# A spectral filter beside an MLP block on one core: two MLP units queued behind chunk work, norms with a guard column, three warm-up products tied to data

## The chip, the cores and the metric

The kernel runs on one core of one Trainium2 chip. TensorE (PE in the profile; PEld are its weight loads) multiplies, VectorE (DVE), ScalarE (ACT) and GpSimd (POOL) do the elementwise work, and SyncE (SP) issues the DMAs. The metric is device time in microseconds of one execution, the median of three runs.

## What is computed

`x` is 2048 x 448. It is layer-normalised to `xn`, and the output is a sum of three things:

```python
xn = layernorm(x)
y  = irfft2(rfft2(xn) * (w_r + 1j * w_i))          # A: spectral filter
h  = gelu(layernorm(xn) @ w1)                      # B: 448 -> 448
x1 = xn + shift(h) @ w2                            # four column groups, rows shifted by +1 -1 +2 -2
h2 = gelu(layernorm(x1) @ w3) @ w4                 # 448 -> 1792 -> 448
out = x + y + x1 + h2
```

## The kernel before

The 2048 rows are kept as 16 blocks of 128 (row `16 a + b` is partition `a` of block `b`), in four groups of four blocks; group 0 holds blocks 14, 15, 0 and 1. Every large product is made in three passes of f16: high by high, high by low and low by high halves of the two operands. The weights are scaled by powers of two that follow from their sum of squares.

The program runs in stages that overlap.

- **Start** (lines 804 to 867). `warm_up(WARM)` (L806) issues 25 products of a zero tile `wsrc`, 512 columns each, into the bank `wps` (L808), before anything is loaded. `norm1` for group 0 (L328) takes statistics on VectorE (L313, L314), an inverse root by an integer trick (L340, L341) and `nm`, the mean times that root with its sign changed (L343), and applies it to the four blocks: blocks 14 on GpSimd, 15 and 0 on VectorE (L353), block 1 on ScalarE (L350). Meanwhile `squares1` sums the squares of `w1` on ScalarE (L243), one column of `m1` for each of four slices. `powers` (L245) makes the scale of a weight: VectorE sums the columns (`pt`, L248), TensorE sums over partitions with a product by `ones` (`pm`, L254, named p1 for w1), VectorE takes the maximum with 2^-58 (L256) so that a zero matrix gives a usable power, takes the exponent (L258) and builds the scale and its inverse (L260, L261). p1 has the transposes of group 0 behind it (`turn_pe`, L404); `turn_copy` brings them to SBUF as a high half on ScalarE (`xT`, L414) and a low half on VectorE (L415); `split_w` makes the first half of w1 on VectorE (L270); `w1_in` multiplies (L454). `powers` is called four times, for w1, w2, w3 and w4.
- **w1 and w2** for the four groups (L466, L502), the second norm (`ln2`, L508), and the split of w3 and w4.
- **MLP** (`mlp`, L787). The 8 pairs of blocks, G = 0 to 7, are worked in 7 units each, (G, 0) to (G, 6), each over 256 columns of the 1792. `front` (L742) makes the unit's first product (22 products, L425, into a bank `pw`), its gelu in place on ScalarE (L749), the high half `hf` on ScalarE (L752), and the low half on VectorE (L753). `back` (L757) makes the second product from `hf` (12 products, L772, into `acc`). Gs 3 to 5 run beside the chunk stage, with the front of one unit ahead of the back of the unit before; two banks hold `pw` in turn.
- **Chunk stage** (L1011 to L1020): 16 chunks of the spectrum. `chunk_a` transforms along the columns (12 products, `pp`, L648) and halves the result (`pf`, L655 on ScalarE, L656 on VectorE). `chunk_b` makes `px` (6 products, L665), copies it crosswise in two halves on ScalarE (`te`, L670) and multiplies by the filter on VectorE (L671, which reads `px`, then L673); GpSimd adds (`z`, L675). `chunk_z` halves z (`zb`, L682 on ScalarE, L683 on VectorE). `chunk_c` transforms back (`pu`, 12 products, L694) and halves (`y`, L697, L698). `px` and `pu` take turns in two banks, so the px of a chunk needs the bank of the px before it.
- **Inverse transform** beside Gs 6 and 7, and the output.

The order on each engine is set by a planner: it simulates the whole program in time and, on each engine, takes the instruction of the best priority among those that are ready. Inside `with prio(EVAC)` the priority is the best there is, so gelu and halves of a unit run as soon as the simulation has them ready. `with behind(key)` adds an edge of order, with no wait of its own: what is issued inside the block comes after the instruction kept under that key in the queue of the same engine. `behind("te", c)` thus means: on ScalarE after the second copy of te of chunk c, on VectorE after L671 of that chunk. Before the change, there is one such pin in `front`, at L751:

```python
with behind("te", 12) if (G, fp) == (4, 1) else contextlib.nullcontext():
    i = A.activation(out=h[:, 0], in_=pm, func=AF.Copy, scale=h3)
    j = V.scalar_tensor_tensor(out=h[:, 1], ...)
```

Of the kernel before, what the change touches and what calls it, by code (L numbers as in the profile page):

```python
# [12 lines left out]
F32 = mybir.dt.float32  # L13
F16 = mybir.dt.float16
I32 = mybir.dt.int32
AF = mybir.ActivationFunctionType
ALU = mybir.AluOpType
AX = mybir.AxisListType
# [5 lines left out]
CS = {b: 4 * g + i for b, (g, i) in WHERE.items()}  # L24
PASS = ((0, 0), (0, 1), (1, 0))
SHIFT = [1, -1, 2, -2]
WARM = 25
ZPRE = 2.0 ** -7
UPRE = 2.0 ** -3
VPRE = 2.0 ** -3  # L30
# [91 lines left out]
def body(tc, nc, x, wf, w1, w2, w3, w4, c_g, c_n, c_small, out):  # L122
    V, A, P, T, SY = nc.vector, nc.scalar, nc.gpsimd, nc.tensor, nc.sync
# [31 lines left out]
    pc = pool("pc")  # L155
# [8 lines left out]
    def xb(b):  # L164
        g, i = WHERE[b]
        return xt[g][:, i]
# [20 lines left out]
    ones = pc.tile([128, 128], F32, name="ones")  # L187
# [51 lines left out]
    def squares(col, src, junk=None):  # L239

        n = src.shape[-1]
        junk = xr.bitcast(F16) if junk is None else junk
        return A.activation(out=junk[:src.shape[0], :n], in_=src, func=AF.Square, scale=2.0 ** -20, accum_out=col)  # L243

    def powers(m, n, key, tag="acc", mid=None):  # L245

        t = pc.tile([128, 2], F32, name=f"pt{key}")
        i = V.tensor_reduce(out=t[:, 0:1], in_=m[:, :n], axis=AX.X, op=ALU.add)  # L248
        after["t" + key] = (i.ins,)
        if mid:  # L250
            with behind("t" + key):
                mid()
        pm = bank(tag, f"pm{key}") if isinstance(tag, str) else tag
        i = T.matmul(pm[:, 0:1], ones, t[:, 0:1], start=True, stop=True)  # L254
        after["p" + key] = (i.ins,)
        V.tensor_scalar(out=t[:, 1:2], in0=pm[:, 0:1], scalar1=2.0 ** -58, scalar2=None, op0=ALU.max)  # L256
        e = pc.tile([128, 3], I32, name=f"pe{key}")
        V.tensor_scalar(out=e[:, 0:1], in0=t.bitcast(I32)[:, 1:2], scalar1=1, scalar2=0x7F800000,  # L258
                        op0=ALU.logical_shift_right, op1=ALU.bitwise_and)
        V.tensor_scalar(out=e[:, 1:2], in0=e[:, 0:1], scalar1=-1, scalar2=185 << 23, op0=ALU.mult, op1=ALU.add)  # L260
        i = V.tensor_scalar(out=e[:, 2:3], in0=e[:, 0:1], scalar1=1, scalar2=69 << 23, op0=ALU.mult, op1=ALU.add)  # L261
        after["s" + key] = (i.ins,)
        return e.bitcast(F32)[:, 1:2], e.bitcast(F32)[:, 2:3]
# [64 lines left out]
    def norm1(g, apply, seen=0, mid=None):  # L328

        bs = GRP[g]  # L330
        n, b0 = len(bs), bs[0]
        stats1(g, range(seen, n))
        mv = mvs[g]
        a = pc.tile([128, 2 * n], F32, name=f"va{b0}")
        yi = pc.tile([128, 2 * n], I32, name=f"vy{b0}")
        y = yi.bitcast(F32)
        with behind(0, 3) if g == 2 else contextlib.nullcontext():
            V.tensor_scalar(out=a[:, n:], in0=mv[:, :n, 1], scalar1=1.0 + EPS, scalar2=EPS * EPS, op0=ALU.mult, op1=ALU.add)
            V.tensor_scalar(out=a[:, 0:n], in0=mv[:, :n, 1], scalar1=EPS, scalar2=None, op0=ALU.add)
        V.tensor_single_scalar(yi, a.bitcast(I32), 1, op=ALU.logical_shift_right)  # L340
        V.tensor_scalar(out=yi, in0=yi, scalar1=-1, scalar2=0x5F3759DF, op0=ALU.mult, op1=ALU.add)  # L341
        nm = pc.tile([128, n], F32, name=f"nma{b0}")
        i = V.scalar_tensor_tensor(out=nm, in0=mv[:, :n, 0], scalar=-1.0, in1=y[:, n:], op0=ALU.mult, op1=ALU.mult)  # L343
        if mid:
            mid()
        for k, b in enumerate(bs):
            y_, m_ = y[:, n + k:n + k + 1], nm[:, k:k + 1]
            if apply[k] is A:
                with behind("sq", g) if ("sq", g) in after else contextlib.nullcontext():
                    i = A.activation(out=xb(b), in_=xb(b), func=AF.Identity, scale=y_, bias=m_)  # L350
                after["na", g] = (i.ins,)
            else:
                i = apply[k].tensor_scalar(out=xb(b), in0=xb(b), scalar1=y_, scalar2=m_, op0=ALU.mult, op1=ALU.add)  # L353
                after["n" if apply[k] is V else "np", g] = (i.ins,)

        q, z = (pc.tile([128, 2 * n], F32, tag=f"v{t}", bufs=2, name=f"v{t}{b0}") for t in "qz")
        w, r = (pc.tile([128, 2 * n], F32, name=f"v{t}{b0}") for t in "wr")
        nm1 = pc.tile([128, n], F32, name=f"nm{b0}")

        def refine():  # L360
            P.tensor_tensor(out=q, in0=y, in1=y, op=ALU.mult)
            P.tensor_tensor(out=q, in0=q, in1=a, op=ALU.mult)
            P.tensor_scalar(out=w, in0=q, scalar1=-10.0 / 3.0, scalar2=None, op0=ALU.add)
            P.tensor_tensor(out=w, in0=w, in1=q, op=ALU.mult)
            P.tensor_scalar(out=w, in0=w, scalar1=5.0, scalar2=None, op0=ALU.add)
            P.tensor_tensor(out=z, in0=w, in1=w, op=ALU.mult)
            P.tensor_tensor(out=z, in0=z, in1=q, op=ALU.mult)
            P.tensor_scalar(out=z, in0=z, scalar1=-0.5 * 0.375 ** 3, scalar2=1.5 * 0.375, op0=ALU.mult, op1=ALU.add)
            P.tensor_tensor(out=r, in0=z, in1=w, op=ALU.mult)

        def gain():
            i = P.tensor_scalar(out=gsc[:, 4 * g:4 * g + 4], in0=r[:, n:], scalar1=r1, scalar2=None, op0=ALU.mult)
            after["g", g] = (i.ins,)

        def scales():
            c, r1st, u = cs[:, 4 * g:4 * g + 4], w[:, 0:n], w[:, n:]
            P.tensor_tensor(out=r1st, in0=r[:, 0:n], in1=y[:, 0:n], op=ALU.mult)
            P.tensor_tensor(out=u, in0=r[:, n:], in1=r[:, n:], op=ALU.mult)
            P.tensor_tensor(out=c, in0=y[:, n:], in1=a[:, n:], op=ALU.mult)
            P.tensor_tensor(out=c, in0=c, in1=u, op=ALU.mult)  # L380
            P.tensor_tensor(out=c, in0=c, in1=r1st, op=ALU.mult)
            P.tensor_scalar(out=c, in0=c, scalar1=s12[:, 0:1], scalar2=None, op0=ALU.mult)
            P.tensor_tensor(out=nm1, in0=mv[:, :n, 0], in1=r1st, op=ALU.mult)
            P.tensor_scalar(out=nm1, in0=nm1, scalar1=-1.0, scalar2=None, op0=ALU.mult)
            for k, b in enumerate(bs):
                xn_scale[b], xn_bias[b] = r1st[:, k:k + 1], nm1[:, k:k + 1]
        return refine, gain, scales

    after = {}

    @contextlib.contextmanager
    def behind(*key):
        key = key if len(key) > 1 else key[0]
        with contextlib.ExitStack() as st:
            for i in after[key]:
                st.enter_context(tc.issue_after(i))
            yield
# [344 lines left out]
    def front(G, fp, tag):  # L742
        tok = slice(256 * (G % 2), 256 * (G % 2) + 256)
        pm = bank(tag, f"pw3_{G}{fp}")
        for ff in range(2):
            f = 2 * fp + ff
            mlp_in(pm[:, 256 * ff:256 * ff + 256], w3p, slice(128 * f, 128 * f + 128), x2all[:, G // 2], tok)
        with prio(EVAC):
            A.activation(out=pm, in_=pm, func=AF.Gelu_apprx_tanh, scale=r3)  # L749
            h = pw.tile([128, 2, 512], F16, tag="hf", bufs=3, name=f"hf{G}{fp}")  # L750
            with behind("te", 12) if (G, fp) == (4, 1) else contextlib.nullcontext():  # L751
                i = A.activation(out=h[:, 0], in_=pm, func=AF.Copy, scale=h3)  # L752
                j = V.scalar_tensor_tensor(out=h[:, 1], in0=pm, scalar=h3, in1=h[:, 0], op0=ALU.mult, op1=ALU.subtract)  # L753
            after["f", G, fp] = i.ins, j.ins
        hs[G, fp] = h
# [50 lines left out]
    def warm_up(n):  # L806
        for i in range(n):
            T.matmul(wps, wsrc[:, 0:128], wsrc, start=True, stop=True)  # L808

    warm_up(WARM)  # L810
    m1, m2, m3, m4 = (pc.tile([128, n], F32, name=f"m{i}") for i, n in ((1, 4), (2, 1), (3, 4), (4, 7)))
    junk4 = row().bitcast(F16)[:, :2 * D]
    V.memset(m1, 0.0)
    V.memset(m2, 0.0)
    xTs = {}
    flat = lambda t: t.rearrange("p a n -> p (a n)")

# [19 lines left out]
    def squares1():  # L837
# [2 lines left out]
            i = squares(m1[:n, t:t + 1], w1s[:n, t])  # L840
        after["sq", 0] = (i.ins,)

    n1 = [norm1(0, [P, V, V, A], mid=squares1)]
    with behind("n", 0):
        s1, r1 = powers(m1, 4, "1", "mm")
    with behind("p1"):
# [19 lines left out]
    with behind("a0", 1):  # L866
        n1.append(norm1(1, [P, V, A, V]))
    with behind("w1", 3):
        squares(m2[:112], flat(w2s[:112]))
    with behind("n", 1):  # L870
        pts = [turn_pe(1, t) for t in range(2)]
        with behind("T", 1):
# [43 lines left out]
    with behind("w2p"):  # L916
        n1[0][2]()
        n1[1][2]()
        for f in n1[2]:
            f()  # L920
    for b in range(2):
        with behind("T", 2):
# [13 lines left out]
    for b in range(2, 4):  # L936
        w2_tile(b)
    turn(3)
    for f in n1[0]:
        f()  # L940
    ln2([0, 1], [A, P])
    with behind("t", 3), behind("h", 2, 3), behind("b0"):
# [124 lines left out]
```

## Time and profile before

| what | us |
|---|---|
| median of 3 runs | 413.87 (413.73 to 414.08) |
| the profiled execution | 413.43 |
| its span, first to last instruction | 411.7 |
| TensorE busy | 406.6 |
| VectorE busy | 295.9 |
| ScalarE busy | 247.4 |
| GpSimd busy | 115.1 |

A line of the profile's timeline gives the start in us from the span's start, the length in us, the engine, the line of the kernel, the operation, what it writes and reads by the program's names, the shape and, after x, how many instructions are merged in it; the bracket behind it is the idle time of the engine just before and what ended it. Products on TensorE are pipelined: the next starts before the end shown for the last, so the spacing of starts is what a product costs. A line of the waits gives the waiting engine, tile and line, what it waited for, the us in total, the number of waits and the longest.

### The profile page before, as it was taken

How to read it: one execution, taken by the hardware profiler on the slowest of the kernel's cores; microseconds unless marked ns; L12 is line 12 of the kernel's file. 1: busy time of each engine (PE TensorE's matmuls, PEld its weight loads, DVE VectorE, ACT ScalarE, POOL GpSimd, SP SyncE). 2: the span in 40 equal slices, each digit the busy share in tenths (PEclk: the TensorE clock that was granted, in tenths of full speed). 3: DMA queues.
4: the chain of work that ended last, by engine and by line, in shares of the span. 5: the costliest groups of instructions: out<-in, count | busy, mean ns of one | idle time of the engine just before them, and what ended most of it. 6: DMA issues, size and time to landing. Idle time of an engine off the chain costs nothing.

```text
span 411.7 us, 8524 instructions
## 1 busy us (share of the span) xinstructions
PE 406.6 (99%) x3310; PEld 290.2 (70%) x3310; DVE 295.9 (72%) x636; ACT 247.4 (60%) x427; POOL 115.1 (28%) x205
## 2 busy tenths in 40 slices
PE   8999999999999999999999999999999999999996
PEld 3555555765677877776887887777776776677885
DVE  5999999897745658863689889875776787667122
ACT  4697979963738766862678888863343434342321
POOL 2987810112307745400031221111212221221000
PEclk9999999999999999999999999999999999999999
DMA  8979599806911283437066555620000213223001
GB/s 280 363 221 199 99 172 328 188 2 140 175 47 48 88 276 129 131 72 164 13 157 170 146 146 141 158 65 2 2 0 2 68 48 110 91 69 133 24 0 46
DMA packets 53496, 48.53 MB, mean 118 GB/s; under 512 B 37600, under 2 KB 48480, under 8 KB 53456
## 3 DMA queue, kind: packets, MB, share of 16 engines
q1 hardware_dynamic: 53456, 47.99, 43.5%
q8 instruction: 26, 0.43, 0.4%
q14 instruction: 14, 0.11, 0.1%
HBM read 35.52 MB, written 3.67 MB: 95 GB/s over the span
## 4 chain that ended last, share of the span: by engine, by line
PE 91%; ACT 4%; DVE 3%; issue 1%; POOL 0%; DVEq 0%; POOLq 0%
PE pw L425 30%; PE acc L772 29%; PE pw L498 9%; PE pw L454 8%; PE ps L591 3%; PE pe L714 2%; PE py L736 2%; PE wps L808 2%; PE pp L648 2%; ACT te L670 2%; PE pu L694 1%; PE px L665 1%; PE pta L404 1%; DVE te L673 1%; ACT zb L682 1%
## 5 line engine op out<-in xcount | busy, mean ns | idle before, releaser
L425 PE MATMUL pw<-x2mem,w3p 128*128 128x256 f16 x1232 | 149.0, 272 | 0.0
L772 PE MATMUL acc<-w4p,hf 128*128 128x448 f16 (+1 forms) x714 | 138.3, 341 | 0.0
L425 PEld LDWEIGHTS <-w3p 128*128 128x128 f16 x1232 | 118.6, 98 | 18.8
L772 PEld LDWEIGHTS <-hf 128*128 128x128 f16 x714 | 69.4, 98 | 48.2 <-DVE hf L753 0.4
L749 ACT ACTIVATE pw<-pw,pe 128x512 f32<-128x512 f32 x56 | 36.8, 656 | 65.6 <-PE pw L425 65.5
L753 DVE SCALAR_TENSOR_TENSOR hf<-pw,h,hf 128x512 f16<-128x512 f32 x56 | 41.8, 749 | 42.6 <-ACT hf L752 42.2
L498 PE MATMUL pw<-w2p,h 112*128 112x448 f16 x192 | 39.1, 352 | 0.0
L752 ACT ACTIVATE hf<-pw,h 128x512 f16<-128x512 f32 x56 | 38.3, 685 | 1.2
L675 POOL TENSOR_TENSOR z<-te 128x450 f32<-128x450 f32 x16 | 16.0, 1000 | 73.7 <-DVE te L673 73.7
L454 PE MATMUL pw<-w1p,xT 128*128 128x448 f16 x176 | 35.1, 352 | 0.3 <-ACT xT L414 0.3
L721 POOL TENSOR_TENSOR e<-e 128x226 f32<-128x226 f32 x16 | 11.3, 707 | 78.2 <-ACT e L718 75.2
L498 PEld LDWEIGHTS <-h 112*128 112x128 f16 x192 | 18.6, 98 | 16.4 <-DMA h<-x2mem 0.3
L454 PEld LDWEIGHTS <-xT 128*128 128x128 f16 x176 | 17.1, 99 | 16.0 <-ACT xT L414 0.5
L655 ACT ACTIVATE pf<-pp 64x450 f16<-64x450 f32 x32 | 17.3, 541 | 15.8 <-PE pp L648 7.8
L718 ACT ACTIVATE e<-pe 128x452 f32<-128x452 f32 x16 | 8.8, 548 | 26.5 <-PE pe L714 26.5
L656 DVE TENSOR_TENSOR pf<-pp,pf 64x450 f16<-64x450 f32 x32 | 19.9, 622 | 5.3 <-ACT pf L655 5.0
L571 POOL TENSOR_TENSOR xr<-xf 128x452 f32<-128x452 f32 x8 | 9.2, 1153 | 31.1 <-issue 27.7
L670 ACT ACTIVATE te<-px 64x450 f32<-64x450 f32 x32 | 17.2, 539 | 0.5
L729 DVE TENSOR_TENSOR vh<-e,vh 128x448 f16<-128x448 f32 x16 | 10.0, 625 | 9.7 <-ACT vh L728 9.7
L574 POOL TENSOR_TENSOR f<-xr 128x452 f32<-128x452 f32 x16 | 16.1, 1028 | 0.6
L582 DVE TENSOR_TENSOR xh<-f,xh 128x452 f16<-128x452 f32 x16 | 11.8, 782 | 5.0 <-ACT xh L581 5.0
L723 DVE TENSOR_TENSOR e<-e 128x113 f32<-128x113 f32 x16 | 9.5, 594 | 7.8 <-POOL e L721 7.8
(169 smaller groups left out, 603.3 us busy)
## 6 DMA issues: line engine op xcount, KB each, us to landing
wc<-wf SPq DMA_DIRECT2D x32, 225.0 KB, 3.7
wl<-wf SPq DMA_DIRECT2D x8, 450.0 KB, 3.8
xf<-x SPq DMA_DIRECT2D x8, 448.0 KB, 3.6
xt<-x SPq DMA_DIRECT2D x3, 896.0 KB, 11.1
w3raw<-w SPq DMA_DIRECT2D x3, 896.0 KB, 14.1
xr<-x SPq DMA_DIRECT2D x12, 224.0 KB, 2.6
out<-xr SPq DMA_DIRECT2D x12, 224.0 KB, 2.0
gn<-c_g SPq DMA_DIRECT2D x16, 128.0 KB, 3.2
```

The costliest lines, as they stand in the source:

```text
L425: T.matmul(ps_out, wp[:, wi + t, cols], xT[:, xi + t, tok], start=t == 0 and wi + xi == 0, stop=t == 3 and wi == 4)
L454: m = T.matmul(pm[:, :D], xTs[g][:, xi + t, 128 * i:128 * i + 128], w1p[:, wi + t], start=t == 0 and p == 0, stop=t == 3 and p == 2)
L498: m = T.matmul(w2b[b][:, :D], hT[g][:112, 4 * hi + k, o:o + 128], w2p[:, wi, k], start=k == 2 and hi + wi == 0, stop=k == 3 and hi == 1)
L574: P.tensor_tensor(out=f[:, :, k:k + 2].rearrange("p b s d -> p s b d"), in0=u[:, :, 0], in1=u[:, :, 1], op=op)
L655: A.activation(out=hi, in_=src, func=AF.Copy)
L656: V.tensor_tensor(out=lo, in0=src, in1=hi, op=ALU.subtract)
L670: i = A.activation(out=e[64 * h:64 * h + 64], in_=px_[64 - 64 * h:128 - 64 * h, :2 * DF], func=AF.Copy)
L675: P.tensor_tensor(out=z, in0=t[:, 0], in1=t[:, 1], op=ALU.add)
L749: A.activation(out=pm, in_=pm, func=AF.Gelu_apprx_tanh, scale=r3)
L752: i = A.activation(out=h[:, 0], in_=pm, func=AF.Copy, scale=h3)
L753: j = V.scalar_tensor_tensor(out=h[:, 1], in0=pm, scalar=h3, in1=h[:, 0], op0=ALU.mult, op1=ALU.subtract)
L772: m = T.matmul(to, h[:, hi, o:o + 128], w4p[0][:, wi, f, r], start=f == 0 and n == 0, stop=f == 13 and n == 2)
```

## The change

It has four parts.

- In `front`, the gelu of unit (4,1) is put behind te 12, as its halves are already; the halves of unit (4,2) are put behind te 14.
- In `powers`, the tiles `m1` to `m4` get one more column, which holds 2^-65 in all 128 partitions; the sum runs over it, so that the sum over partitions holds 128 x 2^-65 = 2^-58 more. The instruction with the maximum (L256) is gone, and the exponent is taken from the bank itself.
- `WARM` is 22 instead of 25. After the first `norm1` there is `warm_on`: a small f32 product of `ones` with the four columns of `nm` into `wps`, and two warm-up products behind it; then the same with the first four columns of the normalised block 0, and one warm-up product behind it.
- `norm1` hands out `nm` as a fourth result, so its users take the first three.

```diff
-WARM = 25
+WARM = 22
     def powers(m, n, key, tag="acc", mid=None):
-        t = pc.tile([128, 2], F32, name=f"pt{key}")
-        i = V.tensor_reduce(out=t[:, 0:1], in_=m[:, :n], axis=AX.X, op=ALU.add)
+        t = pc.tile([128, 1], F32, name=f"pt{key}")
+        i = V.tensor_reduce(out=t, in_=m[:, :n + 1], axis=AX.X, op=ALU.add)
...
-        i = T.matmul(pm[:, 0:1], ones, t[:, 0:1], start=True, stop=True)
+        i = T.matmul(pm[:, 0:1], ones, t, start=True, stop=True)
         after["p" + key] = (i.ins,)
-        V.tensor_scalar(out=t[:, 1:2], in0=pm[:, 0:1], scalar1=2.0 ** -58, scalar2=None, op0=ALU.max)
         e = pc.tile([128, 3], I32, name=f"pe{key}")
-        V.tensor_scalar(out=e[:, 0:1], in0=t.bitcast(I32)[:, 1:2], scalar1=1, scalar2=0x7F800000,
+        V.tensor_scalar(out=e[:, 0:1], in0=pm.bitcast(I32)[:, 0:1], scalar1=1, scalar2=0x7F800000,
                         op0=ALU.logical_shift_right, op1=ALU.bitwise_and)
...
         with prio(EVAC):
-            A.activation(out=pm, in_=pm, func=AF.Gelu_apprx_tanh, scale=r3)
+            with behind("te", 12) if (G, fp) == (4, 1) else contextlib.nullcontext():
+                A.activation(out=pm, in_=pm, func=AF.Gelu_apprx_tanh, scale=r3)
             h = pw.tile([128, 2, 512], F16, tag="hf", bufs=3, name=f"hf{G}{fp}")
-            with behind("te", 12) if (G, fp) == (4, 1) else contextlib.nullcontext():
+            with behind("te", 10 + 2 * fp) if (G, fp) in ((4, 1), (4, 2)) else contextlib.nullcontext():
                 i = A.activation(out=h[:, 0], in_=pm, func=AF.Copy, scale=h3)
...
-    m1, m2, m3, m4 = (pc.tile([128, n], F32, name=f"m{i}") for i, n in ((1, 4), (2, 1), (3, 4), (4, 7)))
+    m1, m2, m3, m4 = (pc.tile([128, n + 1], F32, name=f"m{i}") for i, n in ((1, 4), (2, 1), (3, 4), (4, 7)))
     junk4 = row().bitcast(F16)[:, :2 * D]
-    V.memset(m1, 0.0)
-    V.memset(m2, 0.0)
+    for m, n in ((m1, 4), (m2, 1), (m3, 4), (m4, 7)):
+        V.memset(m, 0.0)
+        V.memset(m[:, n:], 2.0 ** -65)
...
+    def warm_on(src, n):
+
+        after["on"] = (T.matmul(wps[:, 0:4], ones, src, start=True, stop=True).ins,)
+        with behind("on"):
+            warm_up(n)
+
     n1 = [norm1(0, [P, V, V, A], mid=squares1)]
+    warm_on(n1[0][3], 2)
+    warm_on(xb(0)[:, 0:4], 1)
```

More of the change, by code (lines that the diff above doesn't have):

```diff
@@ L386, in scales @@
                 xn_scale[b], xn_bias[b] = r1st[:, k:k + 1], nm1[:, k:k + 1]
-        return refine, gain, scales
+        return refine, gain, scales, nm
     after = {}
@@ L868, in body @@
     with behind("w1", 3):
-        squares(m2[:112], flat(w2s[:112]))
+        squares(m2[:112, 0:1], flat(w2s[:112]))
     with behind("n", 1):
@@ L918, in body @@
         n1[1][2]()
-        for f in n1[2]:
+        for f in n1[2][:3]:
             f()
@@ L938, in body @@
     turn(3)
-    for f in n1[0]:
+    for f in n1[0][:3]:
         f()
```

## The prediction

> **What bounds the kernel now.** I read the page first: busy times and the chain that ended last.
>
> ```profile
> span 411.7 us, 8524 instructions
> ...
> PE 406.6 (99%) x3310; PEld 290.2 (70%) x3310; DVE 295.9 (72%) x636; ACT 247.4 (60%) x427; POOL 115.1 (28%) x205
> ...
> PE 91%; ACT 4%; DVE 3%; issue 1%; POOL 0%; DVEq 0%; POOLq 0%
> ```
>
> TensorE (PE) is the bound nearly everywhere: 5.1 us of the span are not PE. An edit on another engine is worth only the hole it closes in PE's stream, and a product added to that stream is worth its full length. So I next read PE's own waits.
>
> ```profile
> PE wps L808 <- DVE wsrc L186: 1.2, 1, 1.2
> PE pw L454 <- ACT xT L414: 0.3, 1, 0.3
> PE px L665 <- DVE te L671: 0.2, 1, 0.2
> ```
>
> Three waits: before the first warm-up product, before the first w1 product, and one px product behind te on VectorE (DVE). The second and third lie where the change works: the start, and the chunk stage near 260 us. Ends of products are modelled, so a hole can be longer than the idle that is shown; I measure holes from start to start.
>
> **The start.** PE's timeline, and its weight loads (PEld), one per product:
>
> ```profile
> 6.74 0.15 PEld L808 LDWEIGHTS <-wsrc 128*128 128x128 f16 x1 [0.28 <-issue]
> ...
> 7.17 2.05 PEld L808 LDWEIGHTS <-wsrc 128*128 128x128 f16 x10 [0.28 <-issue]
> ```
> ```profile
> 9.33 0.38 PE L808 MATMUL wps<-wsrc 128*128 128x512 f16 x1
> 9.55 0.28 PE L254 MATMUL pm<-pt,ones 128*128 128x1 f32 x2
> 9.69 1.07 PE L404 MATMUL pta<-ident,xt 128*128 128x128 f32 x8
> 11.03 0.35 PE L454 MATMUL pw<-w1p,xT 128*128 128x448 f16 x1 [0.27 <-ACT xT L414]
> ```
>
> A warm-up product takes 0.43 us (6.74 to 7.17) and from 7.17 on a good half of it, 0.22 us (9.33 to 9.55). The 25 end at 9.55, where the norm's product (p1) starts at once; the transposes of x follow at 9.69. What the data did meanwhile, on DVE and ScalarE (ACT):
>
> ```profile
> 7.63 0.16 DVE L343 SCALAR_TENSOR_TENSOR nma<-mva,vy 128x4 f32<-128x4 f32 x1
> 7.83 1.26 DVE L353 TENSOR_SCALAR xt<-xt,vy,nma 128x448 f32<-128x448 f32 x2
> 9.18 0.16 DVE L248 TENSOR_REDUCE pt<-m 128x1 f32<-128x4 f32 x1
> 9.87 0.16 DVE L256 TENSOR_SCALAR pt<-pm 128x1 f32<-128x1 f32 x1 [0.53 <-PE pm L254]
> 10.06 0.15 DVE L258 TENSOR_SCALAR pe<-pt 128x1 int32<-128x1 int32 x1
> ...
> 10.44 0.45 DVE L270 TENSOR_SCALAR w1p<-w1s,pe 128x448 f16<-128x448 f32 x1
> ```
> ```profile
> 10.36 1.08 ACT L414 ACTIVATE xT<-pta 128x512 f16<-128x512 f32 x2 [0.56 <-PE pta L404]
> ```
>
> p1's operand pt is ready at 9.18 + 0.16 = 9.34, so the queue of warm-up products, not the data, is last by 0.21 us. From there the chain is p1, transposes, ACT's copy xT (L414), first w1 product at 11.03.
>
> *The three products that wait.* The total stays 25, but two small f32 products are new: "on" after the 22nd, reading nm, and "on" two products later, reading the normalised block 0. Their price is that of the norm's own two-pass product, which has one moving column where these have four:
>
> ```profile
> 20.36 0.28 PE L254 MATMUL pm<-pt,ones 128*128 128x1 f32 x2
> 20.50 0.35 PE L454 MATMUL pw<-w1p,xT 128*128 128x448 f16 x1
> ```
>
> 0.14 us of PE's stream here (20.36 to 20.50), and 0.14 at 9.55. I take 0.14 each; as a lower bound 0 if PE would have waited for data anyway, as an upper bound 0.28, the row's whole length. Neither product waits: 22 products end at 9.55 - 3 x 0.22 = 8.90, nm was ready at 7.63 + 0.16 = 7.79; first "on" to 9.04; two products to 9.47; block 0 ready at 7.83 + 1.26 = 9.09; second "on" to 9.61; the last product to 9.83. p1 starts at 9.83 instead of 9.55. Queued behind it are the transposes, then ACT's copy, which already waits 0.56 for them, then everything on PE. **+0.28 us** (bounds 0 to +0.56).
>
> If the 22 products ended early, data would bind instead: the second "on" at 9.09, p1 at 9.09 + 0.14 + 0.22 = 9.45, against pt at 9.34 before; the term would be +0.11. I don't take it, since in these rows the queue is last.
>
> The two speeds bear on a rule of the Trainium skill, "TensorE: Matmul & The Clock Gate", section "What's actually happening": PE starts at half clock and is released by an activity window that runs free of the kernel's start, so the switch comes at another time in another execution. The trace agrees on a switch at about half the time (0.43 to 0.22 us); that it moves, no run here shows. By that rule an execution with an earlier switch would have the term +0.11 in place of +0.28, and the sum would be -0.54.
>
> *The maximum removed.* In the four norms DVE loses one instruction between the norm's product and the exponent, 10.06 - 9.87 = 0.19 us each. At the first norm it cannot be seen: the half of w1 (L270) would end at 10.44 + 0.45 - 0.19 + 0.28 = 10.98, ahead of the copy that now lets the w1 product start at 11.03 + 0.28 = 11.31. It hides behind transposes and copy; without that cover it would be worth at most 0.19. The other three norms have no PE wait behind them in the list above: 0. The sum over one more column, and six more memsets on DVE while it still waits for x: 0.
>
> **The chunk stage.** Sixteen pairs of L670 (the two copies of te on ACT), of which the last belongs to chunk 15; counting back, 258.33 is te 12 and 267.70 is te 14. The halves that the old pin puts behind te 12 are those at 259.45: unit (4,1). The next are (4,2).
>
> ```profile
> 257.04 0.66 ACT L749 ACTIVATE pw<-pw,pe 128x512 f32<-128x512 f32 x1
> 257.73 0.58 ACT L682 ACTIVATE zb<-z 128x450 f16<-128x450 f32 x1
> 258.33 1.09 ACT L670 ACTIVATE te<-px 64x450 f32<-64x450 f32 x2
> 259.45 0.69 ACT L752 ACTIVATE hf<-pw,h 128x512 f16<-128x512 f32 x1
> ```
> ```profile
> 265.30 0.69 ACT L752 ACTIVATE hf<-pw,h 128x512 f16<-128x512 f32 x1
> ...
> 267.70 1.09 ACT L670 ACTIVATE te<-px 64x450 f32<-64x450 f32 x2
> ```
> ```profile
> 259.46 0.69 DVE L671 SCALAR_TENSOR_TENSOR te<-px,sc,wc 128x450 f32<-128x450 f32 x1 [0.49 <-ACT te L670]
> ...
> 268.83 0.69 DVE L671 SCALAR_TENSOR_TENSOR te<-px,sc,wc 128x450 f32<-128x450 f32 x1
> 269.43 0.68 DVE L673 SCALAR_TENSOR_TENSOR te<-te,sc,wc 128x450 f32<-128x450 f32 x1
> ```
>
> Each time L671 follows ACT's second copy at once, and its end frees the bank into which PE writes the next px. PE at these two places, with the pitch of its products from the chain of work:
>
> ```profile
> 259.84 0.27 PE L648 MATMUL pp<-csm,y 113*128 113x113 f16 x2
> 260.20 0.55 PE L665 MATMUL px<-pf,gn 128*128 128x225 f16 x4
> ```
> ```profile
> 268.51 0.83 PE L694 MATMUL pu<-gn,zb 128*128 128x128 f16 x12
> 269.57 0.74 PE L665 MATMUL px<-pf,gn 128*128 128x225 f16 x6 [0.22 <-DVE te L671]
> ...
> 270.47 0.35 PE L772 MATMUL acc<-w4p,hf 128*128 128x448 f16 x1
> ```
> ```profile
> 206.26 0.60 PE pp L648 x12
> ...
> 220.80 0.67 PE pu L694 x12
> ```
>
> Two pp products stream in 2 x 0.05 = 0.10, so the hole before 260.20 is 260.20 - 259.84 - 0.10 = **0.26 us**; L671 of te 12 ended at 260.15. Twelve pu products take 0.67, so the hole before 269.57 is **0.39 us**; L671 of te 14 ended at 269.52.
>
> *gelu (4,1) behind te 12.* The activation of 257.04 leaves its place. The zb then needs its sum z from GpSimd (POOL):
>
> ```profile
> 256.05 0.98 POOL L675 TENSOR_TENSOR z<-te 128x450 f32<-128x450 f32 x1 [4.61 <-DVE te L673]
> ```
>
> ready at 257.03, so zb runs at 257.05 and te 12 at about 257.65, 0.68 earlier; L671 ends at about 259.47, before PE's turn at 259.94. The hole goes whole: **-0.26**. Queued behind te 12 are now gelu and halves: te ends at 258.74, gelu to 259.43, halves from 259.45, as before. No price.
>
> *Halves (4,2) behind te 14.* Another 0.69 leaves the ACT queue before te 14, so te 14 starts at 267.0 or earlier and L671 ends by 268.85, before PE's turn at 268.51 + 0.67 = 269.18 (268.92 with the first hole gone): **-0.39**. Price: the halves move from 265.30 to 268.1, DVE's lower half (0.75 us as in this stage) to some 269.6. Waiting for them are the acc products of (4,2), now at 270.47 and due at 269.82 with both holes gone. It fits by 0.2 us: 0, at most +0.3. After that nothing is late next: no PE wait in the list.
>
> **Sum** against the profiled execution (413.43 us, span 411.7): +0.28 - 0.26 - 0.39 = **-0.37 us**. The profiled execution lies 0.44 below the median of 413.87, so I put the difference on the median: **413.5**. That is 0.09%; a measurement of this kernel can tell about 0.2% (0.83 us) from no change, so the likeliest verdict is "same".
>
> **Rivals.**
> 1. *Data, not the queue, sets p1*: the start costs 0 to +0.11 and the time is 413.2 to 413.35. For it: pt was only 0.21 ahead of the queue. Against: the profiled execution had the queue last. Chance 0.10. (The rule of the Trainium skill's "TensorE: Matmul & The Clock Gate" that is weighed above is one way to it.)
> 2. *The halves of (4,2) take the place of the wait removed.* If te 14 doesn't move and DVE takes L673 first, the lower half runs from 270.11 to 270.86 and acc waits from 270.47 - 0.26 = 270.21 on, 0.65 us, while the second hole stays: +0.28 - 0.26 + 0.65 = +0.67, 414.5; half of it, if DVE takes the half first. It decides when the half ends after 269.8. Against: the 0.69 us freed ahead of te 14. Chance 0.12.
> 3. *Slower: a planner's order.* Order on each engine comes from a simulated timeline of the whole program. DVE's norms get shorter and PE's start longer in it, and gelu and halves of the stage's other units may fall ahead of a te elsewhere. Each such place costs a hole like the two measured, 0.26 to 0.39, at most 0.69, the halves' length. One hole eats the forecast gain; four, 4 x 0.33 = +1.3, make 414.8. For it: two of the last three rounds had one without any pin to avoid it. Against: PE shows no other wait after 11 us. Chance 0.23.
> 4. *The same planner's order closes more than the two holes.* To pass -0.83 another 0.46 would have to go; 412.8 with 0.7. PE's shown idle holds no such wait, only holes under modelled ends. Chance 0.13.
> The forecast has 0.42.
>
> **From these to the numbers.** Faster by over 0.2% (under 413.04): rival 4 and a little of rival 1 and the forecast, 0.16. Slower (over 414.70): most of rival 3 and a little of rival 2, 0.22. Same: 0.62. Range 412.7 to 415.0: it holds all but a third of rival 4 and of rival 3 each, some 0.12, and the bounds of the start (0 to +0.56).
>
> **What would show it.** Start right: p1 at 9.83, first w1 product at 11.31; wrong: p1 at 9.55 or before. Maximum right: DVE's e instruction directly after p1, w1 product still released by ACT's xT. Pins right: te 12 about 0.7 earlier against its px, no PE wait on L671, no start-to-start hole ahead of the px of chunks 13 and 15; wrong: a PE wait on hf L753. The prediction falls if PE's order of stages differs from before, or if PE's total of waits after 12 us is above 0.6 us.

## The result and the profile after

The changed kernel takes 413.27 us in the median (22 runs, 412.89 to 413.85), the kernel before in the same comparison 413.89. The ratio is 0.9981, with a 95% interval of 0.9975 to 0.9987: 0.62 us less by the medians, 0.79 by the ratio. Forecast were 413.5 and -0.37: the sign is right, and the gain is larger than forecast, since the interval of the ratio is -0.54 to -1.03 us (a second comparison, f3_changed_again below, gives -0.32). Two of the 22 runs of the kernel before took 415.42 and 415.57, none of the changed kernel's did; the second group of experiments is about such runs. The profiled execution took 413.19.

The page of the changed kernel: span, busy times, the chain that ended last. Its line numbers are one less than before from `powers` on to `front`.

```profile
span 411.4 us, 8535 instructions
...
PE 406.0 (99%) x3314; PEld 290.1 (71%) x3314; DVE 294.4 (72%) x638; ACT 247.7 (60%) x427; POOL 114.6 (28%) x205
...
PE 93%; DVE 3%; DMA 2%; ACT 1%; POOL 1%; issue 0%
```

In the chunk stage the chain no longer runs through te on ScalarE and VectorE; from 250 to 275 us all of it is on PE. PE's waits say the same:

```profile
PE wps L808 <- DVE wsrc L186: 1.2, 1, 1.2
PE wps L846 <- DVE xt L352: 0.5, 1, 0.5
PE pw L453 <- ACT xT L413: 0.3, 1, 0.3
```

The wait of px for te is gone, and the second tie (L846, reading block 0) has one of its own. PE's timeline at the start:

```profile
1.22 6.60 PE L808 MATMUL wps<-wsrc 128*128 128x512 f16 x22 [1.22 <-DVE wsrc L186]
7.94 0.39 PE L846 MATMUL wps<-nma,ones 128*128 128x4 f32 x2
8.18 0.59 PE L808 MATMUL wps<-wsrc 128*128 128x512 f16 x2
9.24 0.39 PE L846 MATMUL wps<-xt,ones 128*128 128x4 f32 x2 [0.47 <-DVE xt L352]
9.48 0.38 PE L808 MATMUL wps<-wsrc 128*128 128x512 f16 x1
9.70 0.28 PE L254 MATMUL pm<-pt,ones 128*128 128x1 f32 x2
9.84 1.07 PE L403 MATMUL pta<-ident,xt 128*128 128x128 f32 x8
11.16 0.93 PE L453 MATMUL pw<-w1p,xT 128*128 128x448 f16 x4 [0.25 <-ACT xT L413]
```

The 22 products end at about 7.7, not at 8.9 as worked out. With 0.43 us for a cold and 0.22 for a warm product, 6.5 us are some 8 cold ones, where the profile of before had 14: the clock opened after 3.4 us here and after 6.0 us there. So in this execution the data bind: the second tie waits for block 0 until 9.24, p1 starts at 9.70 and the first w1 product at 11.16, 0.13 later than before. The two ties take 0.24 us of the stream each (7.94 to 8.18, 9.24 to 9.48), where the sum had 0.14.

The chunk stage, ScalarE at te 12 and te 14, then PE at the px of chunks 13 and 15:

```profile
257.46 0.58 ACT L681 ACTIVATE zb<-z 128x450 f16<-128x450 f32 x1
257.94 1.08 ACT L669 ACTIVATE te<-px 64x450 f32<-64x450 f32 x2
258.92 0.64 ACT L749 ACTIVATE pw<-pw,pe 128x512 f32<-128x512 f32 x1
```
```profile
265.53 0.55 ACT L654 ACTIVATE pf<-pp 64x450 f16<-64x450 f32 x1 [0.77 <-DVE pf L655]
266.13 0.58 ACT L681 ACTIVATE zb<-z 128x450 f16<-128x450 f32 x1
266.73 0.60 ACT L696 ACTIVATE y<-pu 113x512 f16<-113x512 f32 x1
267.35 1.10 ACT L669 ACTIVATE te<-px 64x450 f32<-64x450 f32 x2
268.48 0.69 ACT L752 ACTIVATE hf<-pw,h 128x512 f16<-128x512 f32 x1
```
```profile
259.55 0.83 PE L693 MATMUL pu<-gn,zb 128*128 128x128 f16 x12
260.22 0.55 PE L664 MATMUL px<-pf,gn 128*128 128x225 f16 x4
```
```profile
268.96 0.83 PE L693 MATMUL pu<-gn,zb 128*128 128x128 f16 x12
269.63 0.74 PE L664 MATMUL px<-pf,gn 128*128 128x225 f16 x6
270.21 0.73 PE L772 MATMUL acc<-w4p,hf 128*128 128x448 f16 x3
```

Twelve pu products last 0.67, and px now follows exactly 0.67 behind them, twice (260.22 - 259.55, 269.63 - 268.96): both holes are closed. Te 12 starts 1.63 us behind its own px (256.31), where it was 2.40 (255.93 to 258.33): 0.77 earlier. The acc products of (4,2) run at 270.21 against 270.47 before. The stage gives 0.64 us: the pu ahead of chunk 13's px, at 259.17 before, comes 0.38 later than there, and acc 0.26 earlier. Of the 0.38, 0.13 is the start; most of the rest is a longer wait of a w2 product near 36 us for a transposing DMA (weight loads: 0.5 us instead of 0.3), which the other profiles below show at all lengths between. The span as a whole is only 0.3 us shorter in this pair of profiles.

The wait "0.77 <-DVE pf" on ScalarE, three instructions ahead of te 14, is one that the prediction did not have, and it matters below. So does a new order on PE between the px of chunk 14 and the pu ahead of chunk 15's px, first before, then after:

```profile
265.29 0.74 PE L665 MATMUL px<-pf,gn 128*128 128x225 f16 x6
265.87 0.73 PE L772 MATMUL acc<-w4p,hf 128*128 128x448 f16 x3
266.44 2.24 PE L425 MATMUL pw<-x2mem,w3p 128*128 128x256 f16 x19
```
```profile
265.23 0.74 PE L664 MATMUL px<-pf,gn 128*128 128x225 f16 x6
265.81 0.92 PE L772 MATMUL acc<-w4p,hf 128*128 128x448 f16 x4
266.56 2.56 PE L424 MATMUL pw<-x2mem,w3p 128*128 128x256 f16 x22
```

One acc and three pw products more stand there, so pu comes 3.73 us behind px instead of 3.22 (268.96 - 265.23, 268.51 - 265.29), and the px of chunk 15 is due 0.51 later.

### The profile page after: what moved, and what is told of

Its sections match the earlier page's. It is cut to its first block, busy times and chain, and to the rows that moved or that the text cites. A ratio compares the mean times of both kernels' runs of the same rounds, so it can differ in the third digit from the quotient of the medians.

```text
span 411.4 us, 8535 instructions
## 1 busy us (share of the span) xinstructions
PE 406.0 (99%) x3314; PEld 290.1 (71%) x3314; DVE 294.4 (72%) x638; ACT 247.7 (60%) x427; POOL 114.6 (28%) x205
## 4 chain that ended last, share of the span: by engine, by line
PE 93%; DVE 3%; DMA 2%; ACT 1%; POOL 1%; issue 0%
PE pw L424 33%; PE acc L772 31%; PE pw L497 8%; PE pw L453 6%; PE pu L693 3%; PE ps L590 3%; PE pp L647 2%; PE pe L713 2%; PE px L664 2%; PE py L735 2%; DMA h<-x2mem 1%; DMA xt<-x 1%; DVE sta L312 1%; PE pta L403 1%; DVE xT L414 0%; DVE xt L352 0%
## 5 line engine op out<-in xcount | busy, mean ns | idle before, releaser
L581 DVE TENSOR_TENSOR xh<-f,xh 128x452 f16<-128x452 f32 x16 | 12.7, 833 | 5.0 <-ACT xh L580 5.0
```

## Experiments

Each kernel ran in five rounds beside the kernel before; the before in the three groups of four had medians of 413.68, 413.65 and 413.68. The theory at the start is the prediction's: the gain is the two holes, the start costs something, the norms nothing.

### The parts alone

**e1_pins**: both pins, nothing else.

```diff
-            A.activation(out=pm, in_=pm, func=AF.Gelu_apprx_tanh, scale=r3)
+            with behind("te", 12) if (G, fp) == (4, 1) else contextlib.nullcontext():
+                A.activation(out=pm, in_=pm, func=AF.Gelu_apprx_tanh, scale=r3)
...
-            with behind("te", 12) if (G, fp) == (4, 1) else contextlib.nullcontext():
+            with behind("te", 10 + 2 * fp) if (G, fp) in ((4, 1), (4, 2)) else contextlib.nullcontext():
```

> The kernel before with the two pins alone (gelu of (4,1) behind te 12, halves of (4,2) behind te 14). Theory A (the two holes before the px of chunks 13 and 15 are the whole gain): both holes gone, no other change of the PE stream, -0.65 us, about 413.2. Rival B (the pins gain nothing that lasts, the gain is made at the start): 413.8 to 413.9. Rival C (the gain comes from the norms with fewer instructions): 413.8 to 413.9 as well.

Measured: 413.08, 0.60 less than before. But 3 of its 12 runs took 414.9 to 415.4, with a granted clock of 0.996 (0.999 or 1.000 in the others), so that the ratio is 0.9992 (0.9976 to 1.0008), which alone doesn't exclude 0. Without the runs at a lower clock on either side the medians are 413.02 and 413.65, and both holes are gone from its profile. So theory A holds for the gain, and B and C fall; "no other change of the PE stream" was a miss, for the order on PE changes here as in the changed kernel (1 acc and 3 pw products more ahead of pu). The profiled execution was one of the three, and shows what they are: first a row of PE's waits, then PE's timeline, then the stretch from 12 to 16 us (PEclk is the third number from the end):

```profile
PE pm L254 <- DVE pt L248: 1.3, 1, 1.3
```
```profile
9.81 0.38 PE L254 MATMUL pm<-pt,ones 128*128 128x1 f32 x2 [1.29 <-DVE pt L248]
10.05 1.07 PE L404 MATMUL pta<-ident,xt 128*128 128x128 f32 x8
11.40 1.51 PE L454 MATMUL pw<-w1p,xT 128*128 128x448 f16 x4 [0.27 <-ACT xT L414]
```
```profile
12.00:16.00 4.00, 4.00 (x18) 2.63 (x17) 4.00 (x8) 2.57 (x6) 3.73 (x7) 0.63 1.00 317
```

Here the clock had opened early, the 25 warm-up products were done by 8.4, and PE sat idle for 1.3 us until pt came. Then, with work at hand again, it ran at half clock: four w1 products take 1.51 us where the changed kernel's take 0.93, and the granted clock is 0.63 of full between 12 and 16. In slices of 0.25 us it is 1.00 until 11.50, 0.67 in the next, about 0.5 up to 15.00 and 1.00 after: half clock for 3.4 us, beginning some 1.8 us after p1 started. A clock of 0.996 over 413.1 us is 1.65 us lost, which agrees. That suggested a purpose of the three tied products that the prediction did not see, and the second group tests it.

**e2_start**: 22 products and the two ties, nothing else (the diff's `WARM`, `warm_on` and its two calls).

> The kernel before with the start alone (22 warm-up products, two small products tied to nm and to block 0, three warm-up products behind them). Theory A: two products more in the PE stream, +0.1 (when the clock opens early and data bind) to +0.28 us (when the queue is last), 414.0 to 414.2. Rival B (tying products to data keeps TensorE from something slower in runs without the profiler): faster by 0.3 or more, 413.6 or less. Rival C: 0.

Measured: 413.81, +0.13 (ratio 1.0005, 0.9995 to 1.0015). Theory A's lower end, but the interval, -0.2 to +0.6 us, tells it neither from +0.28 nor from 0 (rival C); B, as a gain of the median, falls. None of the 11 runs is at 0.996; one, of 414.29, is at 0.998.

**e3_guard**: the column and the removed maximum, nothing else.

> The kernel before with the guard column alone (no maximum on VectorE, one more column in the sum). Theory A: the first norm hides behind transposes and copy (0), but the planner's order between 28 and 95 us changes, and the hole of 0.25 us that the profile after shows ahead of 37.28 (a w2 product waiting for the DMA of h) comes with it: 0 to +0.25, 413.9 to 414.1. Rival C (the shorter norms pay): -0.2 to -0.4, 413.5 to 413.7. Rival B: 0.

Measured: 413.62, -0.06 (ratio 0.9995, 0.9984 to 1.0006). The interval, -0.7 to +0.2 us, excludes neither C's gain nor a small price; the profile is sharper. This part alone makes the planner change the order of PE between 60 and 100 us, and of VectorE and ScalarE from some 30 us on. PE is 0.07 later than before at its w1 products (37.02 against 36.95), and still 0.07 later behind the stretch with the new order (acc at 111.67 against 111.60): the shorter norms and the order are together worth nothing there. The hole ahead of 37.02 is 0.10, so the 0.25 ahead of 37.28 in the changed kernel's profile belongs to that execution.

**e4_no_start**: pins and guard.

> The changed kernel without its start: pins and guard, 25 warm-up products as before. Theory A: faster than the changed kernel by 0.1 to 0.28 us, so -0.7 to -0.9 against before by what was measured for the whole change, 413.0 to 413.2. Rival B: slower than the changed kernel, 413.5 or more. Rival C: as the changed kernel, 413.3.

Measured: 413.04, -0.64 (ratio 0.9981, 0.9972 to 0.9989). Theory A, though the changed kernel (413.27) was measured in another comparison. The parts add up, within their intervals: -0.60 + 0.13 - 0.06 = -0.53, against -0.62 for the whole.

### Does the clock fall back?

**f1_warm18**: e4_no_start with fewer products.

```diff
-WARM = 25
+WARM = 18
```

> Pins and guard, and 18 warm-up products with no tie to data (25 before). The one profile of the pins alone that took 414.93 showed TensorE idle for 1.3 us ahead of the first norm's product and its granted clock at 0.63 from 12 to 16 us. Theory D (the clock falls back when TensorE idles between warm-up and data): the warm-up ends at 6.8 to 8.1, the idle time is 1.3 to 2.6 us in every run, so half of the runs or more show a clock of 0.996 and +1.8 us; the median is about 414.8, or there are two groups at 413.0 and 414.8. Rival E (those runs are a disturbance from elsewhere): about one run in eight as before, median 413.0 to 413.1.

Measured: 7 of 12 runs at 0.996 and 414.59 to 415.33, five at 1.000 and 412.91 to 413.36; median 414.64. Theory D. Its profile, one of the seven, PE's waits and the same stretch:

```profile
PE pm L254 <- DVE pt L248: 2.8, 1, 2.8
```
```profile
12.00:16.00 4.00, 4.00 (x19) 2.60 (x18) 3.97 (x9) 2.44 (x6) 3.42 (x7) 0.67 0.99 321
```

**f2_warm15_tied**: the changed kernel with `WARM = 15`, so 18 products in all.

> The changed kernel with 15 products ahead of the first tie in place of 22, so 18 in all: as many as in the run beside it, but three of them wait for data, with two small products. Theory D: the ties cut the idle time into two pieces of about 1 us and the clock is kept in most runs: median 413.2 to 413.4, at most a quarter of the runs at 0.996. Rival E: as the run beside it, 413.1 with one run in eight above.

Measured: 413.42, 2 of 12 runs at 0.996. The two have clocks of 0.995. As many warm-up products as in f1_warm18, but with ties a sixth of the runs instead of seven in twelve: the way that theory D says, though 7 against 2 of 12 could still be chance. Its profile, at a full clock, has pieces of 1.8 and 0.5 us of idle time, not two of about 1:

```profile
8.19 0.39 PE L846 MATMUL wps<-nma,ones 128*128 128x4 f32 x2 [1.76 <-DVE nma L342]
9.49 0.39 PE L846 MATMUL wps<-xt,ones 128*128 128x4 f32 x2 [0.47 <-DVE pt L248]
```

**f3_changed_again** and **f4_pins_start**: the changed kernel once more, and the same without the guard.

> The changed kernel itself, for comparison on the same chip with its variants. Both theories: 413.2 to 413.3; theory D: no run with a clock of 0.996; rival E: one run in eight.

> The changed kernel without the guard: pins and start. If the hole of 0.2 us ahead of 37.3 (the planner's other order between 28 and 95 us) is the guard's price: 413.0 to 413.1, 0.2 less than the changed kernel. If the guard is worth nothing either way: as the changed kernel, 413.2. Theory D: no run at 0.996.

Measured: 413.33 (ratio 0.9990, 0.9981 to 0.9998) and 413.29 (0.9988, 0.9979 to 0.9998), no run at 0.996 in either. The guard is worth nothing that these runs can tell. The changed kernel gains 0.32 here and 0.62 in the first comparison: so wide is the scatter of a difference of medians. In the profile of f3_changed_again the clock opened after 13 cold products; the queue is last there, no tie waits, and p1 starts at 10.04.

### The pins apart, and other starts

**g1_gelu**: the first edit of e1_pins alone. **g2_halves**: the second alone.

> The kernel before with the gelu of (4,1) behind te 12 and no other edit. Theory A: the hole of 0.26 us ahead of the px of chunk 13 goes, and the earlier te 12 carries te 14 some way with it, so that of the 0.39 us ahead of the px of chunk 15 a part goes too: -0.26 to -0.65, about 413.0 to 413.4 where before takes 413.65. If either pin does the whole, one of the two runs stands at 413.0.

> The kernel before with the halves of (4,2) behind te 14 and no other edit; PE's order stays as before. Theory A: only the hole of 0.39 us ahead of the px of chunk 15 goes: -0.3 to -0.39, 413.25 to 413.35; the hole of 0.26 stays.

Measured: 413.01 (-0.67; ratio 0.9988, 0.9969 to 1.0007, with 2 of 11 runs at 0.996) for the gelu, 413.77 (+0.09; ratio 0.9999, 0.9990 to 1.0008) for the halves. The gelu's pin does the whole and the halves' pin nothing, and the profiles, below, say it more sharply than the medians; for the halves the expectation was -0.3 to -0.39 and it is a miss. PE ahead of the px of chunk 15, first with the gelu's pin alone, then with the halves' alone:

```profile
269.34 0.83 PE L694 MATMUL pu<-gn,zb 128*128 128x128 f16 x12
270.01 0.74 PE L665 MATMUL px<-pf,gn 128*128 128x225 f16 x6
```
```profile
269.11 0.83 PE L694 MATMUL pu<-gn,zb 128*128 128x128 f16 x12
270.16 0.55 PE L665 MATMUL px<-pf,gn 128*128 128x225 f16 x4 [0.22 <-DVE te L671]
```

0.67 behind pu, so no hole, against 1.05. With the gelu's pin alone PE's order is again a new one: as in the changed kernel, and three acc products more ahead of pu. With the halves' pin alone it is that of before, and te 14 stays 2.41 behind its px (265.89 to 268.30, as 265.29 to 267.70 before). ScalarE, then VectorE, with the halves' pin alone say why:

```profile
265.23 0.64 ACT L749 ACTIVATE pw<-pw,pe 128x512 f32<-128x512 f32 x1
266.64 0.55 ACT L655 ACTIVATE pf<-pp 64x450 f16<-64x450 f32 x1 [0.77 <-DVE pf L656]
267.21 0.60 ACT L697 ACTIVATE y<-pu 113x512 f16<-113x512 f32 x1
267.70 0.57 ACT L682 ACTIVATE zb<-z 128x450 f16<-128x450 f32 x1
268.30 1.09 ACT L670 ACTIVATE te<-px 64x450 f32<-64x450 f32 x2
```
```profile
264.80 0.69 DVE L671 SCALAR_TENSOR_TENSOR te<-px,sc,wc 128x450 f32<-128x450 f32 x1 [0.40 <-ACT te L670]
265.40 0.68 DVE L673 SCALAR_TENSOR_TENSOR te<-te,sc,wc 128x450 f32<-128x450 f32 x1
265.99 0.61 DVE L656 TENSOR_TENSOR pf<-pp,pf 64x450 f16<-64x450 f32 x1
```

The halves are gone from between gelu and pf, and in their place ScalarE waits 0.77 us for VectorE's half of pf, which stands in VectorE's queue behind te 13. The queue ahead of te 14 was not what set it; te 13 was.

What then closed the hole ahead of chunk 15's px? Two things changed with the gelu's pin, and the rows let each be sized. In the changed kernel te 13 and te 14 come earlier, as te 12 does: L671 of te 14 (L670 there) ends 3.94 us behind the px of chunk 14 (269.17 - 265.23) instead of 4.23 (269.52 - 265.29). And by PE's new order the px of chunk 15 is due 4.40 us behind that px instead of 3.89. By these figures, as an estimate, the earlier te alone would have left about 0.1 of the 0.39 us, and the new order alone nothing; no run has one without the other.

**g3_one_tie**: the second tie only.

```diff
-WARM = 22
+WARM = 23
...
-    warm_on(n1[0][3], 2)
-    warm_on(xb(0)[:, 0:4], 1)
+    warm_on(xb(0)[:, 0:4], 2)
```

> The changed kernel with the second tie alone: 23 warm-up products, one small product that reads block 0, two warm-up products. Theory A: one small product less, 0 to -0.14 against the changed kernel, 413.1 to 413.3. Theory D: the idle time is then in one piece of at most 1 us, with two products and the norm's behind it: no more than one run in twelve at 0.996.

Measured: 413.39, 2 of 11 runs at 0.996. Both are misses: no gain in the median, and 2 runs where one was the most expected. One tie seems to guard the clock less well than two, as far as 11 runs can say.

**g4_warm32**: e4_no_start with `WARM = 32`.

> Pins and guard, and 32 warm-up products with no tie. Theory D: TensorE is never idle before the first norm's product, so no run at 0.996, though nothing is tied to data; the price is that the queue is last by 0.4 to 1.6 us, by when the clock opens: 413.4 to 414.4. Rival E: one run in eight at 0.996.

Measured: 413.69 (413.11 to 414.23), no run at 0.996, for 0.65 more than e4_no_start. This is as theory D says, but weak by itself: at the one run in ten of 25 products, 11 runs show none in one case of three.

All runs together, by the granted clock of each:

| before the first norm's product | runs at 0.996 or 0.995 | of |
|---|---|---|
| 25 products, no tie: before, in the three groups | 10 | 103 |
| 25 products, no tie: e1, e3, e4, g1, g2 | 5 | 56 |
| 22 products and 3 behind two ties: the changed kernel twice, e2, f4 | 0 | 57 |
| 23 products and 2 behind one tie: g3 | 2 | 11 |
| 18 products, no tie: f1 | 7 | 12 |
| 15 products and 3 behind two ties: f2 | 2 | 12 |
| 32 products, no tie: g4 | 0 | 11 |

## Why the prediction was right, and where not

- **The bound: right.** The only edits that moved the time clearly are pins that close holes in PE's stream; the shorter norms, four instructions of VectorE less and a new order between 60 and 100 us, gave -0.06, which is not told from 0.
- **The two holes, -0.65: right in sum** (-0.60 for both pins, -0.67 for the gelu's alone) and seen in the changed kernel's profile. **The split between the pins was wrong.** The step "another 0.69 leaves the ACT queue before te 14, so te 14 starts at 267.0 or earlier" failed: when the halves alone were moved, ScalarE waited for VectorE's pf in their place. An instruction taken out of a queue moves the next one only as far as the next one's own operand, and the prediction looked up that operand (POOL's z) for te 12 and not for te 14, where pf stands before it. The sum held by luck in this part: the gelu's pin brought te 13 and te 14 forward and made the planner put 0.51 us more work ahead of chunk 15's px, and the prediction had neither as a cause of -0.39. Its sign of being wrong, another order on PE, was met between these chunks, and it helped; PE's waits after 12 us, the other sign, are none.
- **The start, +0.28: not settled.** Alone it measured +0.13, and between the changed kernel and e4_no_start 0.23, across two comparisons; the interval of e2_start holds 0 and +0.28 alike. Of the steps, "neither product waits" failed in the changed kernel's profile: p1 starts at 9.70 and the w1 product at 11.16, between the sign for right (9.83, 11.31) and that for wrong (9.55), because the second tie waits 0.47 us for block 0. That is the condition of **rival 1**, whose range of 413.2 to 413.35 holds the measured 413.27; in the profile of f3_changed_again (413.37) the queue is last again. The price of 0.14 for a small product was low: beside 0.14 the profiles show 0.24 or 0.25, for both ties here and for the second in e2_start, f3_changed_again and f4_pins_start. The profiled execution of before was taken for the rule: its clock opened after 14 cold products, that of the changed kernel after 8, that of g1_gelu after 6. That the switch moves between executions is the rule of the Trainium skill, "TensorE: Matmul & The Clock Gate", section "What's actually happening", that the prediction weighed and set aside; the traces now agree, with 14, 8 and 6 cold products.
- **What the prediction lacked: the clock can fall back.** About one run in ten with 25 products and no tie (15 of 159) has a clock of 0.996, against none of 57 with two ties; such runs take 1.3 to 2.5 us more than the others beside them. That idle time ahead of p1 brings it about is borne out by f1_warm18, where more of it gave 7 of 12. The length of the idle time alone does not decide: the clock fell after 1.3 us in e1_pins, and in the profiles of g1_gelu (1.4 us) and f2_warm15_tied (1.8 us) it was kept. What else decides stays open. The Trainium skill, "TensorE: Matmul & The Clock Gate", section "What's actually happening", gives at least one idle window of some 3.4 us as the condition for a cold clock; the two falls that were traced came after 1.3 and 2.8 us, so the measurement goes against the letter of that condition. The 3.4 us at half clock agree with the window's length.
- **Rival 2** (the halves of (4,2) late) came in its order and not in its price: VectorE takes L673 before the lower half, which ends at 270.43, but acc starts at 270.21 without a wait. In `back` the first two products of each three read the high half, and by a pitch of 0.19 us (12 products in 2.27) the third starts at 270.59. **Rival 3** (the planner's order) came in part, through the norms and the pins, and cost nothing. **Rival 4** (more than the two holes) shows in no profile: the chunk stage gained 0.64.

No variant beats the changed kernel clearly. Without the ties the median is 0.2 to 0.3 lower (413.01 to 413.08 against 413.27 to 413.33, across comparisons), but one run in ten pays some 1.9, which is 0.2 in the mean: the ties buy a more even time at the price of the median.

## What to carry to other kernels

Follow a moved instruction to the operand of what comes next in the queue, for each place by itself: a queue slot that comes free is worth nothing if the next instruction waits for another engine anyway. One moved instruction can act on several holes downstream, through its data and through the order that the planner makes of it, so compare the order too before naming a cause. A warm-up of fixed length is right for one moment at which the clock opens; look at more than one execution before taking the end of the warm-up for a fact. When a bound engine idles between warm-up and data, look for runs of a second group with a lower granted clock: as long as they are few, medians don't show them.

## What the runs showed of the hardware

TensorE's clock fell to half after an idle time of only 1.3 us (e1_pins) and 2.8 us (f1_warm18), not during it but 1.6 to 1.8 us after work had begun again, and stayed there for about 3.4 us; the runs with a granted clock of 0.995 or 0.996 took 1.3 to 2.5 us more than the others. Idle times of 1.4 us (g1_gelu) and 1.8 us (f2_warm15_tied) left it at full clock in the executions that were traced. With two ties and 25 warm-up products, where the longest idle piece between first product and p1 was 0.4 to 0.5 us in three profiles and none in a fourth, no run of 57 was at 0.996, and one was at 0.998. At the start the products of 512 columns went from one every 0.43 us to one every 0.22 us after 6 (g1_gelu), 8 (the changed kernel), 13 (f3_changed_again) or 14 (before) of them.
